# Sixteen-bit transposes moved from TensorE to transposing DMAs in a two-path attention kernel

## The chip, the cores and the metric

The kernel runs on one core of a Trainium2 chip. A core has TensorE (PE: matrix products and transposes through the array, with a separate row PEld for the loading of weights), VectorE (DVE), ScalarE (ACT), GpSimd (POOL) and SyncE (SP), which issues the DMAs here. Each engine runs its own instructions in order; semaphores tie the engines together. Products are written to PSUM, everything else lies in SBUF; the inputs, the output and scratch tensors lie in DRAM, and 16 DMA engines move data between DRAM and SBUF. The metric is the device time of one execution in microseconds.

## The reference

The input x has 2048 rows of 640. Two attention paths with 32 heads of 20 columns are computed from it and mixed by a gate per row.

```python
x = A_x
g = _sigmoid((x * gate_w).sum(-1, keepdims=True))
a = _A_ref(x, A_wqkv, A_w_phi, A_wo)
b = _B_ref(x, B_wq, B_wk, B_wv, B_wo, B_beta)
return g * a + (1 - g) * b
```

Path A is linear attention. Each head maps q and k by a 20x20 matrix and takes the softmax of the result and of its negative (40 features); kv and z are sums over all rows, and the output is num/den:

```python
phi_q = jnp.concatenate([_softmax(pq, axis=-1), _softmax(-pq, axis=-1)], axis=-1)
kv = jnp.einsum('bhsf,bhsd->bhfd', phi_k, v)
z = jnp.einsum('bhsf->bhf', phi_k)
o = num / den
```

Path B works in four segments of 512 rows. Inside a segment it is causal softmax attention; beside it stands a memory M, z that collects phi(k) v of the earlier segments, with phi(t) = t + 1 for t > 0 and exp(t) otherwise; both outputs are mixed by a gate per head:

```python
p = _softmax(logits, axis=-1)
a_dot = jnp.einsum('bhqk,bhkd->bhqd', p, vs)
o = g * a_mem + (1.0 - g) * a_dot
M = M + jnp.einsum('bhld,bhle->bhde', pk, vs)
```

Each path ends with a product by its own 640x640 output matrix.

## The kernel before

Rows are cut into 16 chunks of 128 (`sc`), four chunks to a segment (`s`); the 32 heads are handled in 8 groups of four (`g`), a head padded from 20 to 32 columns so that four heads fill 128 partitions. All matrix products with x need x transposed; `xT` holds it whole, 640 columns in five blocks of 128.

**Opening.** The DMAs are issued from SP in the order of the code: the first four chunks of x, the weights `WvA` and `wnat_k`, the rest of x, `wnat_q`, then the weights of path B. `x_transpose` (L207 to L214) turns one chunk: five PE transposes against an identity matrix into one PSUM tile, and one DVE copy into `xT`. `fold_tr` and `fold_mm` multiply the A weights of k, later of q, by `w_phi`.

**Chunk loop of path A (L325 to L336).** For each chunk: `a1_v(sc+2)` (values and the gate logit), `a1_k(sc)` (exponents of both signs on ACT, sums on DVE, the scaling into `EkN` on POOL), the transpose of chunk sc+4, a piece of the q fold from chunk 3 on, and `a1_kv(sc-2)`, which adds to kv and z.

**k and v of path B.** `b_k` (L361) makes one chunk of k: two products of 320 columns, each copied by DVE into the padded `kpad` tile (L369) and, for the first three segments, passed through exp by ACT (`ek`, L372); `phik` is then min(max(k, 0) + 1, exp(k)). `b_v` does the same for the values. Segment 0 is done ahead of the head loop.

**Head loop (L644).** One step k handles head group g of segment s; there are 32 steps, and work of the previous group is woven in. `b_q` makes the transposed q of the next group, with `eq` and `phiq` for the memory; `b_kT` (L409) transposes four 128x128 blocks of `kpad` on PE and copies them to `kT` on DVE (L415). `b_qk` (L420) computes scores in three parts, (chunk 0), (chunks 1 and 3), (chunk 2), into two PSUM tiles `st`; ACT takes the exponent into `PT` (L434) and POOL masks the diagonal blocks (L438). `b_pv` multiplies by the values (`nd`), `b_mem` reads and updates the memory (`am`, `mz`, L454), and `b_epi` writes the group's part of `oB`.

**Fill.** The other work goes between these: `b_k` and `b_v` of the next segment, path A's queries (`a3_pq`, `a3_num`, which ends in `oA`), and the output. `fin_tr` (L547) transposes a block of `oA` or `oB` on PE with a DVE copy into `oT` (L554); `fin_mm` (L557) multiplies ten such pieces by `WoA` and `WoB`, ACT copies the result to `osb`, and SP stores it. Every unit of fill has a position on the axis of steps, made by `place` from a list of knots; in step k, after each third of the scores, all units with a position below k plus 0.37, 0.74 or 1.0 are written out.

**What sets the order.** PE is scheduled by hand: its order is the order of the code. On the other engines and on SP a scheduler sets the order when the program is built, and each engine then keeps it. Four PSUM buffers (tag "w", pool `psw`) serve all products and transposes except the scores and the sums of path A; a product waits until an older user of its buffer has been read.

Of the kernel before, what the change touches and what calls it, by code (L numbers as in the profile page):

```python
# [15 lines left out]
def kernel(  # L16
# [15 lines left out]
    nc = tc.nc  # L32
# [26 lines left out]
    bkw = ctx.enter_context(tc.tile_pool(name="bkw", bufs=2))  # L59
    psw = ctx.enter_context(tc.tile_pool(name="psw", bufs=4, space=PSUM))  # L60
# [14 lines left out]
    x_nat = [apool.tile([P, 4, D], BF16, name=f"x_nat{i}") for i in range(4)]  # L75
# [17 lines left out]
    nc.sync.dma_start(out=x_nat[0][:, 0:2], in_=xv[:, 0:2, :])  # L93
# [4 lines left out]
    nc.sync.dma_start(out=x_nat[0][:, 2:4], in_=xv[:, 2:4, :])  # L98
    wload(WvA[:, :, 0:D], A_wqkv[:, 2 * D:3 * D])
    wload(wnat_k, A_wqkv[:, D:2 * D])  # L100
    for i in range(1, 4):
        nc.sync.dma_start(out=x_nat[i], in_=xv[:, 4 * i:4 * i + 4, :])
# [3 lines left out]
    wq_st = []  # L106
    for c in range(KC):
        w = a1w.tile([P, D], BF16, name="wq_st", bufs=2)
        nc.sync.dma_start(out=w, in_=B_wq[c * P:(c + 1) * P, :])
        wq_st.append(w)  # L110
    wload(WoA, A_wo)
    wload(WoB, B_wo)
    nc.sync.dma_start(out=beta_b, in_=B_beta.partition_broadcast(P))
# [33 lines left out]
    kpad2, phik2, vB2 = [], [], []  # L147
    for b in range(2):
        kp = bres.tile([P, 4, H, 32], BF16, name=f"kpad{b}")
        pk = bres.tile([P, 4, H, 32], BF16, name=f"phik{b}")  # L150
        vb = bres.tile([P, 4, H, V1], BF16, name=f"vB{b}")
        nc.gpsimd.memset(kp[:, :, :, DH:32], 0.0)
        nc.gpsimd.memset(pk[:, :, :, DH:32], 0.0)
        nc.gpsimd.memset(vb[:, :, :, DH:V1], 1.0)
        kpad2.append(kp)
        phik2.append(pk)
        vB2.append(vb)
# [49 lines left out]
    def x_transpose(sc):  # L207
        tp = wtile("xtp", BF16)
        for c in range(KC):
            nc.tensor.transpose(out=tp[:, c * P:(c + 1) * P],  # L210
                                in_=x_nat[sc // 4][:, sc % 4, c * P:(c + 1) * P],
                                identity=ident_b)
        nc.vector.tensor_copy(out=xT[:, :, sc * P:(sc + 1) * P],
                              in_=tp[:, 0:D].rearrange("p (c k) -> p c k", k=P))  # L214
# [110 lines left out]
    for sc in range(NCH):  # L325
        if sc + 2 < NCH:
            a1_v(sc + 2)
        a1_k(sc)
        if sc + 4 < NCH:
            x_transpose(sc + 4)  # L330
        if 3 <= sc < 3 + NG6:
            fold_tr(fq, sc - 3)
        if 9 <= sc < 9 + KC:
            fold_mm(fq, sc - 9)
        if sc >= 2:
            a1_kv(sc - 2)  # L336
# [24 lines left out]
    def b_k(s, c):  # L361
        kp, pk = kpad2[s % 2], phik2[s % 2]
        sc = 4 * s + c
        ek = bkw.tile([P, D], BF16, name="ek")
        rk = bkw.tile([P, D], BF16, name="rk", bufs=1)
        for hf in range(2):
            ps = wtile("kb_ps")
            mm_x(ps[:, 0:320], sc, WkB, 320 * hf, 320 * hf + 320)
            nc.vector.tensor_copy(out=kp[:, c, hf * 16:hf * 16 + 16, 0:DH],  # L369
                                  in_=ps[:, 0:320].rearrange("p (h d) -> p h d", d=DH))  # L370
            if s < NSEG - 1:
                nc.scalar.activation(out=ek[:, hf * 320:hf * 320 + 320], in_=ps[:, 0:320],  # L372
                                     func=ACT.Exp)
        if s < NSEG - 1:
            nc.vector.tensor_scalar(out=rk.rearrange("p (h d) -> p h d", d=DH),
                                    in0=kp[:, c, :, 0:DH], scalar1=0.0, scalar2=1.0,
                                    op0=ALU.max, op1=ALU.add)
            nc.vector.tensor_tensor(out=pk[:, c, :, 0:DH],
                                    in0=rk.rearrange("p (h d) -> p h d", d=DH),
                                    in1=ek.rearrange("p (h d) -> p h d", d=DH), op=ALU.min)  # L380
# [9 lines left out]
    def b_q(s, g):  # L390
        ps = wtile("qb_ps")
        for c in range(KC):
            nc.tensor.matmul(ps, lhsT=WqB[:, c, 4 * g:4 * g + 4, :],  # L393
                             rhs=xT[:, c, s * L:(s + 1) * L],
                             start=(c == 0), stop=(c == KC - 1))
        qT = bw.tile([P, L], BF16, name="qT", bufs=2)
        nc.vector.tensor_copy(out=qT, in_=ps)  # L397
        phiq = None
        if s > 0:
            eq = bw.tile([P, L], BF16, name="eq", bufs=1)  # L400
            nc.scalar.activation(out=eq, in_=ps, func=ACT.Exp)  # L401
            rq = bw.tile([P, L], BF16, name="rq")
            nc.vector.tensor_scalar(out=rq, in0=qT, scalar1=0.0, scalar2=1.0,
                                    op0=ALU.max, op1=ALU.add)
            phiq = bw.tile([P, L], BF16, name="phiq", bufs=3)
            nc.vector.tensor_tensor(out=phiq, in0=rq, in1=eq, op=ALU.min)
        return qT, phiq

    def b_kT(s, g):  # L409
        ps = wtile("kT_ps", BF16)  # L410
        for c in range(4):
            nc.tensor.transpose(out=ps[:, c * P:(c + 1) * P],
                                in_=kpad2[s % 2][:, c, 4 * g:4 * g + 4, :], identity=ident_b)
        kT = bw.tile([P, L], BF16, name="kT", bufs=2)
        nc.vector.tensor_copy(out=kT, in_=ps[:, 0:L])  # L415
        return kT
# [37 lines left out]
    def b_mem(s, g, phiq):  # L454
        tm = None
        if s > 0:
            am = wtile("am_ps")
            for j in range(4):
                nc.tensor.matmul(am[:, j * 84:(j + 1) * 84], lhsT=phiq[:, j * P:(j + 1) * P],
                                 rhs=Mbd[:, g].rearrange("p i e -> p (i e)"), start=True, stop=True)  # L460
            tm = b_norm(am, s, g, Cm, "m")
        if s < NSEG - 1:
            mz = wtile("mz_ps")
            for c in range(4):
                nc.tensor.matmul(mz[:, 0:84], lhsT=phik2[s % 2][:, c, 4 * g:4 * g + 4, :],
                                 rhs=vB2[s % 2][:, c, 4 * g:4 * g + 4, :],
                                 start=(c == 0), stop=(c == 3))
            nc.vector.tensor_tensor(out=Msb[:, g], in0=mz[:, 0:84].rearrange("p (i e) -> p i e", e=V1),
# [24 lines left out]
    segs = [Seg() for _ in range(NSEG)]  # L493

# [12 lines left out]
    def a3_num(s, qc, half):  # L507
# [33 lines left out]
        if qc == 0 and half == 0:  # L541
            segs[s].oA = boA.tile([P, 4, D], BF16, name="oA", bufs=3)
        nc.gpsimd.tensor_tensor(  # L543
            out=segs[s].oA[:, qc, h0 * DH:(h0 + nh) * DH].rearrange("p (h d) -> p h d", d=DH),
            in0=ts[:, 0, 0:nh, :], in1=ts[:, 1, 0:nh, :], op=ALU.add)

    def fin_tr(s, qc, X):  # L547
        o = segs[s].oA if X == 0 else segs[s].oB
        tp = wtile("otp", BF16)
        for k5 in range(KC):  # L550
            nc.tensor.transpose(out=tp[:, k5 * P:(k5 + 1) * P], in_=o[:, qc, k5 * P:(k5 + 1) * P],  # L551
                                identity=ident_b)
        oT = bw.tile([P, KC * P], BF16, name=f"oT{X}")
        nc.vector.tensor_copy(out=oT, in_=tp[:, 0:D])  # L554
        segs[s].oT[qc, X] = oT

    def fin_mm(s, qc, hf):  # L557
# [5 lines left out]
        for X, Wo in enumerate((WoA, WoB)):  # L563
            for k5 in range(KC):
                nc.tensor.matmul(ps[:, 0:320], lhsT=segs[s].oT[qc, X][:, k5 * P:(k5 + 1) * P],  # L565
# [27 lines left out]
    def fill_fin(s):  # L593
        tr = [[(0.3, lambda qc=qc, X=X: fin_tr(s, qc, X)) for X in range(2)] for qc in range(4)]
        mm = [[(0.68, lambda qc=qc, hf=hf: fin_mm(s, qc, hf)) for hf in range(2)]
              for qc in range(4)]
        u = tr[0] + []
        for qc in range(4):
            for hf in range(2):
                if qc < 3:  # L600
                    u.append(tr[qc + 1][hf])
                u.append(mm[qc][hf])
        return u
# [17 lines left out]
    for s, (p0, p1) in enumerate(((9.01, 17), (17.01, 25), (25.4, 32))):  # L621
        fill += place(fill_fin(s), ((0, p0), (1, p1)))
    fill.sort(key=lambda v: v[0])

    first = fill_bkv(0)
    for t, (_, u) in enumerate(first):
        u()
        if t == 1:
            a1_kv(NCH - 2)
        if t == 4:  # L630
            a1_kv(NCH - 1)
            a1_state()
# [8 lines left out]
    cur = (b_q(0, 0), b_kT(0, 0))  # L641
    prev = None
    SHARE = (0.37, 0.74, 1.0)
    for k in range(NG):  # L644
        s, g = divmod(k, G)
        if g == 0:
            segs[s].oB = boA.tile([P, 4, D], BF16, name="oB")
            segs[s].oT = {}
        (qT, phiq), kT = cur
        PT = bpt.tile([P, 4, 1280], BF16, name="PT")  # L650
        nd = None
        for t, cs in enumerate(((0,), (1, 3), (2,))):
            b_qk(qT, kT, PT, cs)
            if t == 0 and k + 1 < NG:
                nq = b_q(*divmod(k + 1, G))
            if t == 1 and k + 1 < NG:
                nxt = (nq, b_kT(*divmod(k + 1, G)))
            if prev is not None:
# [6 lines left out]
                else:  # L665
                    b_pv(ps_, pg_, pPT, [3], nd)
                    b_epi(ps_, pg_, nd, tm, segs[ps_].oB)
            while fill and fill[0][0] < k + SHARE[t]:
                fill.pop(0)[1]()
        prev = (s, g, PT, phiq)  # L670
        if k + 1 < NG:
            cur = nxt
    ps_, pg_, pPT, pphi = prev
# [4 lines left out]
    for _, u in fill_fin(NSEG - 1):  # L678
        u()
# [29 lines left out]
```

The softmax here doesn't subtract the row's maximum and nothing guards it: scores larger than these inputs give would overflow.

## Time and profile before

| | before |
|---|---|
| median time | 439.85 us (four runs, 438.72 to 439.86) |
| profiled span | 438.1 us |
| busy PE, ACT, DVE, POOL | 363.4, 274.7, 261.0, 210.4 us |
| mean granted TensorE clock | 0.941 |
| DRAM read and written | 9.21 and 2.62 MB |
| x_transpose, 16 chunks | 80 PE transposes, 16 DVE copies (median 492 ns) |
| kT, 32 groups | 128 PE transposes, 32 DVE copies (416 ns) |
| output blocks, 32 | 160 PE transposes, 32 DVE copies (483 ns) |

A page of the profile gives busy time per engine, the span in 40 equal slices (digits are tenths busy), the chain of work that ended last, followed back from the last instruction, and groups of instructions with their busy time, mean duration and the idle time of their engine before them. Matrix products overlap in the array, so the duration of one (219 ns for a transpose) is longer than the distance from one to the next. "A <- B" in the table of waits means that engine A stood idle until B was done. "issue" is idle time for which the profile shows no cause. A name such as `L551` is line 551 of the kernel before.

### The profile page before, as it was taken

What the parts mean: (1) busy time and instruction counts of PE and PEld (TensorE: products, weight loads), DVE (VectorE), ACT (ScalarE), POOL (GpSimd) and SP (SyncE); (2) the same over time, 40 slices, a digit from 0 to 9 for tenths busy, and PEclk for the clock granted to TensorE, in tenths of its full rate; (3) what the DMA queues carried; (4) which work ended last, traced back from release to release, by engine and by line L of the source; (5) the groups of instructions that cost most, each with busy time, mean ns of one, the idle gap of its engine ahead of it and who ended that gap; (6) DMA issues with size and microseconds to landing.
All of it is one profiled execution on the core that took longest, in us unless ns stands there. A gap on an engine that the chain in (4) does not pass through costs nothing.

```text
span 438.1 us, 10470 instructions
## 1 busy us (share of the span) xinstructions
PE 363.4 (83%) x4257; PEld 235.2 (54%) x4289; DVE 261.0 (60%) x680; ACT 274.7 (63%) x515; POOL 210.4 (48%) x365
## 2 busy tenths in 40 slices
PE   1899999797987687788988888898886788787686
PEld 1677877573454343455655455564554454445365
DVE  6477766896367453677665566665666456555431
ACT  1566666525687466777766677676676886765502
POOL 9047776950355444544463434554354545444510
PEclk9999999989899796899998999999999998988669
DMA  8960000000000000000000000000000000000001
GB/s 250 363 224 9 4 1 1 1 0 1 2 0 2 2 1 0 1 2 2 16 4 14 16 2 16 1 16 2 17 16 1 16 1 16 17 2 15 13 14 51
DMA packets 10610, 12.49 MB, mean 29 GB/s; under 512 B 1347, under 2 KB 10563, under 8 KB 10563
## 3 DMA queue, kind: packets, MB, share of 16 engines
q1 hardware_dynamic: 10563, 11.83, 8.2%
q8 instruction: 33, 0.54, 0.5%
q14 instruction: 14, 0.11, 0.1%
HBM read 9.21 MB, written 2.62 MB: 27 GB/s over the span
## 4 chain that ended last, share of the span: by engine, by line
PE 52%; ACT 19%; DVE 14%; POOL 9%; issue 4%; DMA 2%; SPq 0%; POOLq 0%; DVEq 0%; ACTq 0%
ACT PT L434 12%; PE o_ps L565 10%; PE pq_ps L500 6%; PE qb_ps L393 5%; PE vb_ps L231 4%; PE st L428 4%; PE va_ps L231 4%; PE kb_ps L231 4%; PE nd_ps L448 4%; POOL PT L438 3%; PE ka_ps L231 3%; DVE ts L538 2%; PE acc L271 2%; PE otp L551 2%; ACT eq L401 2%
## 5 line engine op out<-in xcount | busy, mean ns | idle before, releaser
L434 ACT ACTIVATE PT<-st 128x1024 bf16<-128x1024 f32 (+1 forms) x192 | 158.7, 885 | 21.7 <-PE st L428 19.6
L438 POOL TENSOR_SCALAR_AFFINE_SELECT PT<-PT 128x512 bf16<-128x512 bf16 x128 | 80.7, 642 | 114.6 <-ACT PT L434 98.8
L231 PEld LDWEIGHTS <-xT 128*128 128x128 bf16 x640 | 62.0, 100 | 32.3 <-issue 6.8
L428 PE MATMUL st<-qT,kT 32*128 32x128 bf16 (+3 forms) x512 | 44.5, 311 | 15.2 <-ACT PT L434 13.0
L397 DVE CAST qT<-qb_ps 128x512 bf16<-128x512 f32 x32 | 22.1, 691 | 46.0 <-PE qb_ps L393 45.9
L259 POOL TENSOR_TENSOR EkN<-Ek,krec 128x1280 bf16<-128x1280 bf16 x16 | 37.9, 2366 | 18.8 <-DVE krec L258 17.3
L448 PE MATMUL nd_ps<-vB,PT 128*128 128x21 bf16 x1280 | 42.4, 173 | 4.9 <-DVE ts L538 2.0
L448 PEld LDWEIGHTS <-PT 128*128 128x128 bf16 x1280 | 38.2, 97 | 10.8 <-POOL rr L529 3.8
L393 PE MATMUL qb_ps<-xT,WqB 128*128 128x512 bf16 x148 | 42.0, 404 | 1.8 <-DVE ts L538 0.8
L543 POOL TENSOR_TENSOR oA<-ts 128x360 bf16<-128x360 f32 (+1 forms) x32 | 27.6, 861 | 31.1 <-DVE ts L538 27.6
L565 PEld LDWEIGHTS <-oT 128*128 128x128 bf16 x320 | 31.5, 104 | 15.4 <-issue 1.7
L500 PE MATMUL pq_ps<-xT,WqA 128*128 128x512 bf16 x100 | 32.4, 420 | 8.6 <-DVE ts L538 3.1
L569 ACT CAST osb<-o_ps 128x320 bf16<-128x320 f32 x32 | 13.6, 426 | 39.5 <-PE o_ps L565 39.3
L428 PEld LDWEIGHTS <-kT 32*128 32x128 bf16 x512 | 14.0, 92 | 42.1 <-issue 37.1
L503 ACT ACTIVATE Eq<-pq_ps 128x512 bf16<-128x512 f32 x24 | 14.3, 597 | 28.6 <-PE pq_ps L500 28.4
L565 PE MATMUL o_ps<-WoA,oT 128*128 128x320 bf16 x160 | 29.9, 322 | 2.1 <-DVE ts L538 1.4
L518 PE MATMUL num_ps<-KVZ,Eq 128*128 128x132 bf16 (+1 forms) x192 | 18.5, 220 | 15.1 <-DVE ts L538 5.8
L231 PE MATMUL vb_ps<-WvB,xT 128*128 128x320 bf16 x160 | 27.2, 319 | 3.7 <-DVE ts L538 2.3
L538 DVE TENSOR_TENSOR ts<-num_ps,cs 128x360 f32<-128x360 f32 (+1 forms) x64 | 28.2, 483 | 1.9 <-DVE cs L533 0.2
L565 PE MATMUL o_ps<-WoB,oT 128*128 128x320 bf16 x160 | 28.9, 314 | 0.0
L241 ACT CAST vA<-va_ps 128x320 bf16<-128x320 f32 x32 | 13.7, 427 | 22.0 <-PE va_ps L231 22.0
L251 ACT ACTIVATE Ek<-ka_ps 128x320 bf16<-128x320 f32 x64 | 23.0, 439 | 5.5 <-PE ka_ps L231 4.9
(114 smaller groups left out, 669.0 us busy)
## 6 DMA issues: line engine op xcount, KB each, us to landing
out_dram<-osb SPq DMA_DIRECT2D x16, 160.0 KB, 1.8
x_nat<-in_A_x_dram SPq DMA_DIRECT2D x3, 640.0 KB, 9.1
WvA<-in_A_wqkv_dram SPq DMA_DIRECT2D x1, 800.0 KB, 5.5
wnat_k<-in_A_wqkv_dram SPq DMA_DIRECT2D x1, 800.0 KB, 7.3
wnat_q<-in_A_wqkv_dram SPq DMA_DIRECT2D x1, 800.0 KB, 11.3
WkB<-in_B_wk_dram SPq DMA_DIRECT2D x1, 800.0 KB
WvB<-in_B_wv_dram SPq DMA_DIRECT2D x1, 800.0 KB, 11.5
wq_st<-in_B_wq_dram SPq DMA_DIRECT2D x5, 160.0 KB, 7.6
```

The costliest lines, as they stand in the source:

```text
L231: nc.tensor.matmul(ps, lhsT=xT[:, c, sc * P:(sc + 1) * P], rhs=W[:, c, lo:hi], start=(c == 0), stop=(c == KC - 1))
L251: nc.scalar.activation(out=Ek[:, sgn, 320 * hf:320 * hf + 320], in_=ps[:, 0:320], func=ACT.Exp, scale=1.0 if sgn == 0 else -1.0)
L259: nc.gpsimd.tensor_tensor(out=EkNs[sc % 4][:, 0:1280].rearrange("p (h f) -> p h f", f=DH), in0=Ek.rearrange("p s (h f) -> p (s h) f", f=DH ...
L393: nc.tensor.matmul(ps, lhsT=WqB[:, c, 4 * g:4 * g + 4, :], rhs=xT[:, c, s * L:(s + 1) * L], start=(c == 0), stop=(c == KC - 1))
L428: nc.tensor.matmul(st2[i // 2][:, i % 2, o:o + n], lhsT=kT[r:r + 32, c * P:(c + 1) * P], rhs=qT[r:r + 32, c * P:L], start=True, stop=True, ...
L434: nc.scalar.activation(out=PT[:, 2 * pr:2 * pr + 2, base:base + w], in_=st2[pr][:, :, 0:w], func=ACT.Exp, scale=SCALE_B)
L438: nc.gpsimd.affine_select(out=view, in_=view, pattern=[[0, 4], [1, P]], compare_op=ALU.is_ge, fill=0.0, base=0, channel_multiplier=-1)
L448: nc.tensor.matmul(nd[:, j * 84 + i * V1:j * 84 + (i + 1) * V1], lhsT=PT[:, i, o:o + P], rhs=vb[:, c, 4 * g + i, :], start=(j == 0 and i = ...
L500: nc.tensor.matmul(ps, lhsT=WqA[:, c, g * 120:g * 120 + P], rhs=xT[:, c, s * L:(s + 1) * L], start=(c == 0), stop=(c == KC - 1))
L538: nc.vector.tensor_tensor(out=ts[:, sgn, 0:nh, :], in0=pss[sgn][:, :, 0:DH], in1=cs[:, sgn, 0:nh, None].to_broadcast([P, nh, DH]), op=ALU. ...
L543: nc.gpsimd.tensor_tensor(out=segs[s].oA[:, qc, h0 * DH:(h0 + nh) * DH].rearrange("p (h d) -> p h d", d=DH), in0=ts[:, 0, 0:nh, :], in1=ts ...
L565: nc.tensor.matmul(ps[:, 0:320], lhsT=segs[s].oT[qc, X][:, k5 * P:(k5 + 1) * P], rhs=Wo[:, k5, hf * 320:hf * 320 + 320], start=(n == 0), s ...
```

## The change

The purpose is to take transposes of 16-bit data off PE, with their PSUM buffers and DVE copies, and to have them made by the DMA engines, which can transpose a block on its way from DRAM to SBUF.

- **x.** Chunks 4 to 15 are read from DRAM by 12 transposing DMAs straight into `xT`. Chunks 0 to 3 stay on PE. The five `wq_st` loads and `beta_b` move up in the queue, ahead of these DMAs; `wnat_q` and the B weights follow them.
- **kT.** `b_k` writes its padded chunk (128x1024) to a DRAM scratch `kd` and reads it back transposed into `kT2`, which holds the 8 groups of one segment; there are two of them, and three rotating `kpad` chunks. `b_kT` is gone.
- **Output blocks.** `o_put` stores 128x640 blocks of `oA` and `oB` to the scratch `od`, `o_get` reads them back transposed into `oT`, 0.8 step ahead of the first product that uses them. For the last segment `oB` is still transposed on PE; its `oA` goes by DMA. The knots of the output work of the three segments in the loop begin 0.4 to 0.8 step later.
- **Exponents.** `ek` and `eq` read the 16-bit copies in SBUF instead of PSUM; `ek` is one instruction of 640 columns instead of two.
- **Memory.** `am` and `mz` share one PSUM bank; both products come before the normalisation.

```diff
-    for i in range(1, 4):
-        nc.sync.dma_start(out=x_nat[i], in_=xv[:, 4 * i:4 * i + 4, :])
+    for sc in range(4, NCH):
+        nc.sync.dma_start_transpose(out=xT[:, :, sc * P:(sc + 1) * P],
+                                    in_=x2[sc * P:(sc + 1) * P, :])
     wload(wnat_q, A_wqkv[:, 0:D])
...
-        if sc + 4 < NCH:
-            x_transpose(sc + 4)
...
-        kp, pk = kpad2[s % 2], phik2[s % 2]
+        kp, pk = kpads[(4 * s + c) % 3], phik2[s % 2]
...
-            if s < NSEG - 1:
-                nc.scalar.activation(out=ek[:, hf * 320:hf * 320 + 320], in_=ps[:, 0:320],
-                                     func=ACT.Exp)
+        rows = slice(c * P, (c + 1) * P)
+        nc.sync.dma_start(out=kd[s][rows, :], in_=kp.rearrange("p h d -> p (h d)"))
+        nc.sync.dma_start_transpose(out=kT2[s % 2][:, :, rows], in_=kd[s][rows, :])
         if s < NSEG - 1:
+            nc.scalar.activation(out=ek.rearrange("p (h d) -> p h d", d=DH), in_=kp[:, :, 0:DH],
+                                 func=ACT.Exp)
...
-            nc.scalar.activation(out=eq, in_=ps, func=ACT.Exp)
+            nc.scalar.activation(out=eq, in_=qT, func=ACT.Exp)
...
+        am = wtile("am_ps")
         if s > 0:
-            am = wtile("am_ps")
...
+        if s < NSEG - 1:
+            mz = am[:, 336:420]
...
+    def o_put(s, X, qc, src):
+        nc.sync.dma_start(out=od[s][X][qc * P:(qc + 1) * P, :], in_=src)
+
+    def o_get(s, X, qc):
+        rows = slice(qc * P, (qc + 1) * P)
+        oT = bw.tile([P, KC, P], BF16, name=f"oT{X}", bufs=4)
+        nc.sync.dma_start_transpose(out=oT, in_=od[s][X][rows, :])
+        segs[s].oT[qc, X] = oT
...
-    for s, (p0, p1) in enumerate(((9.01, 17), (17.01, 25), (25.4, 32))):
-        fill += place(fill_fin(s), ((0, p0), (1, p1)))
+    for s, (p0, p1) in enumerate(((9.8, 17.2), (17.8, 25.2), (25.8, 32))):
+        fin = place(fill_fin(s), ((0, p0), (1, p1)))
+        fill += fin
+        for X in range(2):
+            fill += [(max(fin[2 * qc][0] - 0.8, 8 * s + 8.7),
+                      lambda s=s, X=X, qc=qc: o_get(s, X, qc)) for qc in range(4)]
...
+    for qc in range(4):
+        o_get(NSEG - 1, 0, qc)
     ps_, pg_, pPT, pphi = prev
     tm = b_mem(ps_, pg_, pphi)
     nd = wtile("nd_ps")
     b_pv(ps_, pg_, pPT, [0, 1, 2, 3], nd)
     b_epi(ps_, pg_, nd, tm, segs[ps_].oB)
-    for _, u in fill_fin(NSEG - 1):
-        u()
+    fin_tr(NSEG - 1, 0)
+    for qc in range(4):
+        if qc < 3:
+            fin_tr(NSEG - 1, qc + 1)
+        for hf in range(2):
+            fin_mm(NSEG - 1, qc, hf)
```

## The prediction

> **What bounds the kernel now.** I read the busy shares and the chain of waits first, then the stretches by stage, then who waits for whom, then the timeline around the instructions that the change touches.
>
> ```profile
> PE 363.4 (83%) x4257; PEld 235.2 (54%) x4289; DVE 261.0 (60%) x680; ACT 274.7 (63%) x515; POOL 210.4 (48%) x365
> DMA  8960000000000000000000000000000000000001
> PE 52%; ACT 19%; DVE 14%; POOL 9%; issue 4%; DMA 2%; SPq 0%; POOLq 0%; DVEq 0%; ACTq 0%
> ```
>
> TensorE (PE) is the fullest engine and half of the chain that ends last. The DMA engines are idle after slice 3. By stage (columns: stretch and length, then busy us of PE, PEld, DVE, ACT, POOL, then granted clock, DMA share, GB/s):
>
> ```profile
> 24.00:84.00 60.00, 57.91 (x714) 45.49 (x711) 44.87 (x75) 40.32 (x112) 44.58 (x64) 1.00 0.10 30
> 84.00:103.00 19.00, 17.14 (x165) 12.02 (x167) 15.69 (x35) 3.93 (x11) 9.21 (x20) 0.91 0.01 2
> 103.00:417.00 314.00, 258.19 (x3130) 155.65 (x3158) 184.43 (x539) 218.43 (x368) 144.12 (x255) 0.93 0.02 8
> 417.00:438.00 21.00, 16.31 (x141) 11.80 (x137) 4.73 (x11) 3.41 (x8) 1.34 (x2) 0.84 0.09 32
> ```
>
> The chunk loop of path A (24 to 84) is filled by PE. The head loop (103 to 417, 32 steps of 314/32 = 9.8 us) has PE at 82% and ACT at 70%; its 56 us of PE idle time is the question. What PE waited for there:
>
> ```profile
> PE st L428 <- ACT PT L434: 13.0, 25, 1.4
> PE num_ps L518 <- DVE ts L538: 5.8, 3, 3.7
> PE num_ps L518 <- ACT eq L401: 5.1, 5, 1.0
> ```
>
> The other waits on `ACT eq` are 1.8, 1.0, 0.9 and 0.8 us, so 9.6 us in all; on the copies of kT and oT 0.9, 0.8, 0.3, 0.2 and 0.6, so 2.8 us; on `DVE ts` 16.9 us. These are PSUM buffers that come free late: the four "w" buffers are shared by every product and every transpose.
>
> **What the Trainium skill says.** "VectorE: DVE Perf Modes", section "The three transpose paths": a 128x128 bf16 transpose takes 390 ns on TensorE and 1309 ns by DMA. The TensorE figure is a latency: here five transposes in a row delay the next product by 0.28 us (timeline below), 56 ns each. "Advanced Engine Details and Errata", section "X-Bar Transpose (TRN2)": transposing DMAs are as fast as ordinary ones. "DMA: Bandwidth & Descriptors", section "Latency and other measured facts": 261 GB/s measured for a transposing DMA. The trace of before holds no transposing DMA, so nothing here confirms or denies the three. "SBUF — State Buffer", section "Who interferes with whom": a VectorE copy in a two-port mode and a GpSimd instruction exclude each other for the whole instruction. The trace agrees: a copy of 4 columns took 6.08 us while GpSimd ran its memsets.
>
> **Part 1: x transposed by DMA (chunks 4 to 15).** Removed: 12 groups of five transposes and 12 copies of 0.492 us on DVE.
>
> ```profile
> 428.65 0.44 PE L551 MATMUL otp<-ident_b,oA 128*128 128x128 bf16 x5
> 428.93 0.84 PE L565 MATMUL o_ps<-WoA,oT 128*128 128x320 bf16 x5
> ```
>
> From start to start the group costs PE 0.28 us. 12 x 0.28 = 3.4 us. A chunk lasted about 4.2 us, and GpSimd works 2.36 + 1.10 us of it with about 0.25 us between, so its floor is 3.7 us and it takes back a little: I take 3.0 us. Added: 12 transposing DMAs of 160 KB, then `wnat_q`, on one queue. The loads ahead of them are 3.0 MB, which at the 364 GB/s of 10 to 20 us and with the start end near 13 us. The next ones cost 160 KB / 261 GB/s = 0.63 us each at least (estimate from the DMA page) and 5 x 1.309 = 6.5 us at most (estimate from the VectorE page, blocks one after the other). Deadlines: chunk 4 is read after `a1_k(1)`, about 27 us; `wnat_q` is read by PE at 34.2 us in PE's own order, so a late one stops everything. With 2.5 us for its 800 KB, twelve transposes have (34.2 - 2.5 - 13)/12 = 1.55 us each before PE stands still. I take 0.63: two pages say it, and 1309 ns for 32 KB looks like a fixed latency, as 160 KB of output here takes 1.8 us to land. Then the last lands near 22 us and DMA costs nothing.
>
> The start: `beta_b` now comes early and in the built program DVE has `sig_b` ahead of `ident_b`, so the first four PE transposes wait for it. Before, DVE was held anyway:
>
> ```profile
> 5.47 6.08 DVE L135 CAST ind<-bd 128x4 bf16<-128x4 f32 x1
> 8.66 3.06 DVE L310 COPY WvA<-gtp 128x5 bf16<-128x5 bf16 x1
> ```
>
> They end when the memsets do (11.5 us). The kpad memsets shrink from two (1.37 + 1.69 us) to three of a quarter of the size, about 1.0 us together: 2 us less. DVE then starts near 9.5 us with 0.23 + 0.91 us more to do and five copies into WqB that wait for their loads (near 13 us). I take 0, within 2 us either way.
>
> **Part 2: kT by DMA.** Removed: 32 groups of four transposes, 0.24 us of PE each (253.63 to 253.87 us), and 32 DVE copies of 0.416 us. In the loop 31 x 0.24 = 7.4 us of PE and 12.9 us of DVE. Added: 16 writes of 256 KB to DRAM, each followed by a transposing DMA that waits for it on the in-order SP queue. The path is about 0.4 us issue, 1.8 us landing (as `out_dram<-osb`), 0.4 us issue, 1.8 + 1.0 us: 5.4 us. Segments 1 to 3 have their last k chunk about 2.9 steps (28 us) ahead. Segment 0 is the narrow one: its chunk 3 leaves DVE at 100.0 us and is needed by the second score group, 106.57 us before. It just fits; up to 3 us lost.
>
> **Part 3: output blocks by DMA.** Removed: seg 0 to 2, 24 groups x 0.28 = 6.7 us of PE and 24 copies x 0.485 = 11.6 us of DVE; in the tail four groups, 1.1 us. Added: put, wait, get on SP. The get of oB comes at step 8s+8.7, the first final product at 8s+9.8: about 10 us for a 5 us path. In the tail the four oA gets are queued before the last head's work and oB stays on PE, so no round trip stands at the end. SP is in order: a get that waits for its put holds the stores queued behind it, and ACT waits for a store only when both `osb` buffers are out, two blocks later (18 us). I cost these at 2 us.
>
> **Part 4: eq and ek read SBUF; am and mz share a bank.** `eq` no longer holds the PSUM buffer of q: the 9.6 us of PE waits on it are open to saving, I take half, since the next buffer may be late too: 4.8 us. `ek` becomes one instruction of 640 instead of two of 320: from 439 ns (320) and 597 (512) a slope of 0.82 ns, so 0.70 instead of 0.88 us, 12 times, 2 us of ACT beside other work. One bank fewer per head; b_norm of `am` now waits for four more products (0.15 us), nothing.
>
> **Sum.** Loop: PE loses (7.4 + 6.7)/0.93 clock = 15.2 us of work; as PE is busy 82% of the stage, that share counts: 12.5. Copies' waits 2.8; `ts` waits fall with DVE's load, 24.5 of 184 us: 13% of 16.9 = 2.2; eq 4.8. Less 2 + 3 for new waits: 17.3. With the opening 3.0 and the tail 1.1: 21.4, so 439.85 - 21.4 = 418.5 us.
>
> **The rivals.**
> - A, off the path: the loop is really set by the circle of scores, exponent (ACT, 70%), mask and value product. For: `ACT PT` is the largest wait of PE and the largest line of the chain, 12%. Against: only 13 of 56 us of idle time. Then a third of the loop's gain comes: 439.85 - 3 - 1.1 - 5.8 = 430.
> - B, the transposing DMA is slow (1.309 us a block): x takes 78 us, `wnat_q` lands near 94 instead of 33, so the opening is 57 us longer; segment 0's kT, 4 x 10.5 us, adds some 25; a segment needs 4 x 10.5 + 8 x 6.5 = 94 us of DMA against 78 of loop, 15 more. About 530 us. For: the one block price there is. Against: two pages' bandwidths.
> - C, new waits through the in-order queue: 12 output blocks each stop PE 2 us, four segment starts 1 us, and 0 at the start turns into 2: 418.5 + 30 = about 448, slower than before. For: every get stands behind a wait of 2 us, about 44 of them. Against: leads of one step and more.
>
> **How the numbers follow.** Forecast 0.56, A 0.20, B 0.11, C 0.12, and 0.01 for no change between them. Faster 0.76, same 0.02, slower 0.22. The range begins at 404 (all PE work and all waits on eq gained, no new wait: 15.2 + 2.8 + 9.6 + 2.2 in the loop and 4.5 elsewhere give 405.5) and ends at 446, below which lie A and the milder half of C; B and the rest are the 2 in 10 left out.
>
> **What would show it.** Right: no PE wait on a DMA over 2 us; the time between first chunks falls from 4.2 to near 3.9 us; the score loop's PE busy time falls by 14 to 17 us; waits on eq nearly gone; transposing DMAs under 1.5 us apart on SP. Wrong: PE idle at `wnat_q` near 34 us or at xT, long rows "PEld oT <- DMA" or "kT <- DMA", ACT waiting at `osb`, or a head loop as long as before with ACT fuller. A granted clock below 0.93 in the loop would eat the gain without any of these.

## The result and the profile after

| | before | after |
|---|---|---|
| median of all runs | 437.97 us (16 runs, 436.58 to 439.86) | 411.57 us (10 runs, 408.12 to 412.46) |
| ratio, 95% interval | | 0.9386 [0.9364, 0.9409] |
| profiled span, mean clock | 438.1 us, 0.941 | 409.8 us, 0.942 |

The change makes the kernel 6.1% faster, 26.4 us between the medians, 28.3 between the profiled spans. The forecast was 418.5 us; the range 404 to 446 holds the time. A ratio leaves out an execution that took over 1.5% more than the fastest one of its kernel, which here is one run, 435.11 us of e1. Line numbers in a profile are those of that run's own kernel. The busy shares, the slices of the DMA engines and the chain that ended last, of the page of after:

```profile
PE 341.1 (83%) x3930; PEld 216.0 (53%) x3961; DVE 231.2 (56%) x608; ACT 271.4 (66%) x503; POOL 209.3 (51%) x366
DMA  7989000035120122236112115621110152100411
PE 54%; ACT 20%; POOL 11%; DVE 9%; issue 4%; POOLq 0%; DVEq 0%; ACTq 0%
```

PE lost 22 us and DVE 30, but PE is still at 83%: the span shrank with it. The DMA engines, idle after slice 3 before, are now in use to the end, though far from full. PE has 31 records fewer than PEld (3930 against 3961; before 4257 against 4289). Each product loads its weights once (in the head loop of e7 below both counts are 2927), so these are missing records, in both traces about equally many, and the difference of the two PE times can be used.

To place the time I cut both executions at the same events: the first product `ka`, the first `kb`, the first score `st`, the first transpose `otp` of the tail. Stretches of before, then of after (stretch and length, busy us of PE, PEld, DVE, ACT, POOL, granted clock, DMA share, GB/s):

```profile
22.70:85.80 63.10, 60.25 (x749) 47.44 (x748) 45.98 (x76) 41.21 (x114) 46.14 (x69) 1.00 0.12 37
85.80:102.60 16.80, 15.72 (x136) 10.86 (x135) 14.74 (x34) 3.93 (x11) 7.64 (x15) 0.90 0.01 2
102.60:417.40 314.80, 258.96 (x3145) 156.20 (x3177) 184.43 (x539) 218.43 (x368) 144.51 (x255) 0.93 0.02 8
417.40:438.10 20.70, 15.91 (x125) 11.40 (x121) 4.73 (x11) 3.41 (x8) 0.94 (x2) 0.83 0.09 32
```

```profile
22.80:81.90 59.10, 56.71 (x689) 44.01 (x687) 39.04 (x56) 40.73 (x113) 45.73 (x68) 1.00 0.28 83
81.90:97.00 15.10, 13.90 (x136) 10.00 (x135) 13.10 (x33) 3.54 (x7) 8.08 (x16) 1.00 0.44 123
97.00:389.90 292.90, 243.20 (x2902) 142.57 (x2932) 164.98 (x484) 215.83 (x360) 145.00 (x255) 0.93 0.24 61
389.90:409.80 19.90, 15.12 (x106) 10.16 (x102) 2.89 (x7) 3.41 (x8) 0.90 (x2) 0.81 0.18 51
```

| stage | before | after | difference |
|---|---|---|---|
| start to first ka | 22.7 | 22.8 | +0.1 |
| chunk loop of path A (ka to kb) | 63.1 | 59.1 | -4.0 |
| k and v of segment 0 (kb to st) | 16.8 | 15.1 | -1.7 |
| head loop (st to tail's otp) | 314.8 | 292.9 | -21.9 |
| tail | 20.7 | 19.9 | -0.8 |

The k and v of segment 0 ran at a clock of 0.90 before and 1.00 after. Over all the runs this stretch follows the clock and not the place where kT is made: 15.1 to 15.6 us at 1.00 (15.3 in e1, which still has every transpose on PE), 16.2 at 0.94, 16.8 and 16.9 at 0.90. So most of its 1.7 us is no gain of the change. The head loop's PE busy time fell from 258.96 to 243.20 us (-15.8) and PE's idle time in it from 55.8 to 49.7 (-6.1); the granted clock is 0.93 in both. PE's largest waits in the head loop of after (waiting line, releaser: us in all, times, longest):

```profile
PE st L426 <- ACT PT L432: 18.7, 36, 1.9
PE num_ps L522 <- DVE ts L542: 5.1, 2, 4.0
PE qb_ps L400 <- DVE ts L542: 2.6, 3, 1.4
PE vb_ps L238 <- DVE Msb L470: 2.4, 3, 1.3
...
PE num_ps L522 <- DVE Msb L470: 1.3, 1, 1.3
```

The rows on `eq` and on the copies of kT and oT are gone. No row of PE names a DMA: every transpose by DMA was in time. Part of the gain was given back in two other rows: the exponent `PT` (13.0 before, 18.7 now) and `Msb`, which was 0.5 us and is 4.5 now, two rows of 0.4 that are not shown included. The memory's sum now lies in the bank of `am`, and that buffer stays taken until DVE has added it to `Msb`.

The queue itself, first its three transposing lines (ns min/median/max on SP, first and last start), then median us from issue to landing:

```profile
L111 SPq DMA_TRANSPOSE xT<-in_A_x_dram x12: 1276/1276/2657, 8.5 to 26.0; - x12
L378 SPq DMA_TRANSPOSE kT<-kd x16: 1232/1232/1677, 86.2 to 296.6; - x16
L559 SPq DMA_TRANSPOSE oT<-od x28: 1199/1202/1980, 149.2 to 390.2; - x28
```
```profile
kd<-kpad SPq DMA_DIRECT2D x16, 256.0 KB, 2.5
od<-oA SPq DMA_DIRECT2D x16, 160.0 KB, 1.8
oT<-od SPq DMA_TRANSPOSE x28, 2.8
kT<-kd SPq DMA_TRANSPOSE x16, 3.2
xT<-in_A_x_dram SPq DMA_TRANSPOSE x12, 3.9
```

A transposing DMA holds SP for 1.2 us or more, about the same for 160 and 256 KB, where an ordinary one mostly takes 0.3 to 0.6 us, and in the median lands 2.8 to 3.9 us after its issue.

### The profile page after: what moved, and what is told of

Same layout as the page of the kernel before. It is cut to its first block, busy times and chain, and to the rows that moved or that the text cites. A ratio compares the mean times of both kernels' runs of the same rounds, so it can differ in the third digit from the quotient of the medians.

```text
span 409.8 us, 9889 instructions
## 1 busy us (share of the span) xinstructions
PE 341.1 (83%) x3930; PEld 216.0 (53%) x3961; DVE 231.2 (56%) x608; ACT 271.4 (66%) x503; POOL 209.3 (51%) x366
## 3 DMA queue, kind: packets, MB, share of 16 engines
q1 hardware_dynamic: 59091, 29.41, 28.1%
## 4 chain that ended last, share of the span: by engine, by line
PE 54%; ACT 20%; POOL 11%; DVE 9%; issue 4%; POOLq 0%; DVEq 0%; ACTq 0%
ACT PT L432 15%; PE o_ps L579 11%; PE qb_ps L400 6%; PE va_ps L238 5%; PE st L426 5%; PE vb_ps L238 5%; PE pq_ps L504 5%; PE ka_ps L238 4%; PE kb_ps L238 4%; POOL PT L436 4%; PE nd_ps L446 3%; PE acc L278 3%; DVE ts L542 1%; DVE qT L404 1%; ACT osb L583 1%
## 5 line engine op out<-in xcount | busy, mean ns | idle before, releaser
L432 ACT ACTIVATE PT<-st 128x1024 bf16<-128x1024 f32 (+1 forms) x192 | 158.5, 884 | 18.9 <-PE st L426 17.5
L238 PEld LDWEIGHTS <-xT 128*128 128x128 bf16 x640 | 60.8, 99 | 30.4 <-DVE Msb L470 2.9
L426 PE MATMUL st<-qT,kT 32*128 32x128 bf16 (+3 forms) x512 | 48.5, 311 | 21.3 <-ACT PT L432 18.7
L446 PEld LDWEIGHTS <-PT 128*128 128x128 bf16 x1280 | 36.7, 96 | 14.1 <-issue 6.4
L579 PEld LDWEIGHTS <-oT 128*128 128x128 bf16 x320 | 32.4, 105 | 19.9 <-issue 4.1
L426 PEld LDWEIGHTS <-kT 32*128 32x128 bf16 x512 | 15.7, 92 | 50.9 <-issue 47.9
L479 DVE RECIPROCAL rd<-nd_ps 128x16 f32<-128x16 f32 x32 | 8.0, 249 | 36.9 <-PE nd_ps L446 36.9
L263 DVE TENSOR_REDUCE ksum<-Ek 128x64 f32<-128x1280 bf16 x16 | 23.7, 1482 | 8.2 <-ACT Ek L258 7.6
L400 PEld LDWEIGHTS <-WqB 128*128 128x128 bf16 x160 | 13.9, 101 | 23.3 <-issue 12.9
```

The source lines that it names most:

```text
L238: nc.tensor.matmul(ps, lhsT=xT[:, c, sc * P:(sc + 1) * P], rhs=W[:, c, lo:hi], start=(c == 0), stop=(c == KC - 1))
L400: nc.tensor.matmul(ps, lhsT=WqB[:, c, 4 * g:4 * g + 4, :], rhs=xT[:, c, s * L:(s + 1) * L], start=(c == 0), stop=(c == KC - 1))
L426: nc.tensor.matmul(st2[i // 2][:, i % 2, o:o + n], lhsT=kT[r:r + 32, c * P:(c + 1) * P], rhs=qT[r:r + 32, c * P:L], start=True, stop=True, ...
L432: nc.scalar.activation(out=PT[:, 2 * pr:2 * pr + 2, base:base + w], in_=st2[pr][:, :, 0:w], func=ACT.Exp, scale=SCALE_B)
L446: nc.tensor.matmul(nd[:, j * 84 + i * V1:j * 84 + (i + 1) * V1], lhsT=PT[:, i, o:o + P], rhs=vb[:, c, 4 * g + i, :], start=(j == 0 and i = ...
L579: nc.tensor.matmul(ps[:, 0:320], lhsT=segs[s].oT[qc, X][:, k5, :], rhs=Wo[:, k5, hf * 320:hf * 320 + 320], start=(n == 0), stop=(n == 2 * ...
```

## The experiments

The theory: PE's transposes and the PSUM buffers and copies that they held were on the path of the head loop, and the DMAs hide. The rivals: the gain came from one small part (the x opening, or `eq`); only one of the three freed resources counts; the queue is near the path. Unless said otherwise, a difference is the difference of two ratios (0.9386 for the changed kernel) times the time of before in the same call (438.35 to 439.22 us). Nothing of the computation is left out in any of these kernels.

### Parts alone, on the kernel before

`eq` alone (e1), which reads the copy instead of PSUM:

```diff
-            nc.scalar.activation(out=eq, in_=ps, func=ACT.Exp)
+            nc.scalar.activation(out=eq, in_=qT, func=ACT.Exp)
```

> The kernel before with one line changed: eq reads qT in SBUF instead of the PSUM buffer of q. Theory of the prediction: half of the 9.6 us that PE waited on eq comes back, 4.8 us faster than before. Rival: the next buffer is late as well and the wait only moves, less than 1 us.

Measured: 0.9812 [0.9749, 0.9875], 8.2 us faster than before. This rests on three runs (427.22 to 431.85 us) that had clocks of 0.948 to 0.951, where before had 0.937 to 0.949. At like clocks the gain is 5 to 6 us: 430.56 and 431.85 at 0.948 against 436.73 at 0.949, and 435.11 against 440.09, both at 0.937. All of part 4 (e2): beside `eq`, one `ek` from SBUF and `mz = am[:, 336:420]`.

> The kernel before with the whole of part 4 (eq and ek read SBUF, am and mz share a bank), every transpose still on PE. Theory: about 5 us faster, nearly all from eq. Rival: sharing the bank frees a PSUM buffer per head as well, 8 us or more.

Measured: 435.55 us, 0.9936 [0.9915, 0.9957], 2.8 us faster, where 5 was expected. So `ek` with the shared bank gives back part of what `eq` alone brings: 5.4 us by the ratios (the two intervals leave 2.5 to 8.3), about 3 at like clocks. The profiles agree: PE is idle for 46.3 us of the head loop in e1 and for 50.1 in e2. Which of the two does it wasn't separated; PE's waits on `Msb`, 1.1 us in e1 and 3.7 in e2, speak for the bank. Part 1 alone (e3), x by DMA, with its order of loads:

```diff
-        if sc + 4 < NCH:
-            x_transpose(sc + 4)
+    for sc in range(4, NCH):
+        nc.sync.dma_start_transpose(out=xT[:, :, sc * P:(sc + 1) * P],
+                                    in_=x2[sc * P:(sc + 1) * P, :])
```

> The kernel before with part 1 alone (x chunks 4 to 15 by transposing DMAs, loads reordered). Theory: 12 groups of transposes on PE, 3.4 us, and nothing lost to the queue: 3 to 4 us faster than before. Rival: the later start of the first transposes and the loads behind the DMAs take it back, under 1.5 us.

Measured: 436.52 us, 0.9932 [0.9904, 0.9959], 3.0 us faster, as expected. Its chunk loop is 4.0 us shorter, as in the changed kernel, but its first `ka` comes 1.8 us later than before (24.5). The two parts make 5.8 of about 27 us, which leaves some 21 for kT and the output blocks.

### Parts undone, on the changed kernel

kT back on PE (e4), with `b_kT` and its DVE copy in place of `kd`; the output blocks back on PE (e5), with `fin_tr` for both paths and the old knots:

```diff
-        nc.sync.dma_start(out=kd[s][rows, :], in_=kp.rearrange("p h d -> p (h d)"))
-        nc.sync.dma_start_transpose(out=kT2[s % 2][:, :, rows], in_=kd[s][rows, :])
...
+                nxt = (nq, b_kT(*divmod(k + 1, G)))
```

> The changed kernel with kT made on PE and copied by DVE again, no scratch for k. Theory: 7.4 us of PE at clock 0.93 in the head loop, all of it counting now that the stage lost 15.8 us of PE work and 21.9 us of time, with some waits on buffers, and 1.3 us ahead of the loop: 9 to 11 us slower than the changed kernel. Rival: the narrow deadline of segment 0 and the trips through the queue ate part of the gain: under 6 us slower.

> The changed kernel with all output blocks transposed on PE and copied by DVE again, with the old positions of this work. Theory: 6.7 us of PE at clock 0.93 in the loop, some waits on buffers and 1.1 us in the tail: 8 to 10 us slower than the changed kernel. Rival: the put and get in one queue cost as much as they save: under 4 us slower.

Measured: e4 424.88 us, 0.9711 [0.9657, 0.9764], 14 us slower than the changed kernel; e5 423.12 us, 0.9652 [0.9603, 0.9702], 12 us slower. Both lie above what was expected. In the head loop of e4 PE is busy for 7.2 us more than in e7, the same loop without products added and with every PE record there (see below), and the loop is 12.0 us longer; in e5 it is 6.4 and 7.9. So beside the PE work waits came back, more of them with kT. The two make 26 us together against 21 left after parts 1 and 4; with some 3 us of uncertainty on each, this doesn't show that the parts help each other.

### Which freed resource counts

Each transposed block freed three things: PE time, DVE time, one turn of a "w" buffer. Three kernels put one of them back into the changed kernel, at the same 56 places, beside the q and the output products and not where the old transposes stood, with results that nothing uses: PE time (e6: four idle products of 128 columns for each q, five for each of 24 output products, in tiles that are there anyway), DVE time (e7: 56 reductions) and buffers (e11: a product of 4 columns into a tile of its own, and a copy of 4 columns).

```diff
+            nc.tensor.matmul(ps[:, c * P:(c + 1) * P], lhsT=ident_b, rhs=ident_b,
+                             start=True, stop=True)
```
```diff
+            nc.vector.tensor_reduce(out=dd, in_=qT[:, 0:352], axis=AX.X, op=ALU.max)
```
```diff
+        sl = wtile("sl")
+        nc.tensor.matmul(sl[:, 0:4], lhsT=ident_b, rhs=ind, start=True, stop=True)
+        sd = bw.tile([P, 4], F32, name="sd", bufs=4)
+        nc.vector.tensor_copy(out=sd, in_=sl[:, 0:4])
```

> The changed kernel with only the PE time of the removed transposes put back: four idle 128x128 products ahead of each q product and five ahead of each output product of the first three segments, into buffers that are overwritten at once; no further PSUM buffer, no DVE copy. Theory that PE work itself counts: 14.1 us at clock 0.93, 12 to 15 us slower than the changed kernel. Rival, that the buffers and copies counted: under 6 us slower.

> The changed kernel with only the DVE time of the removed copies put back: a reduction of 352 elements after each q copy and one of 320 at each output product of the first three segments, about 0.42 us each, 56 in all, read by nobody. Theory: DVE at 56% of the loop has room, 2 to 4 us slower than the changed kernel. Rival, that DVE's queue delayed PE's buffers: 8 us slower or more.

> The changed kernel with only the PSUM buffers of the removed transposes put back: at each of the 56 places one product of 4 columns into a buffer of its own and a DVE copy of 4 columns that frees it. Theory: 2 to 5 us slower than the changed kernel. Rival, that the four shared buffers were the real bound: 8 us slower or more.

| put back | median us | ratio [95%] | slower than the changed kernel by |
|---|---|---|---|
| PE time | 424.93 | 0.9633 [0.9574, 0.9692] | 10.8 us |
| DVE time | 419.16 | 0.9541 [0.9482, 0.96] | 6.8 us |
| buffer turns | 426.5 | 0.9684 [0.9629, 0.974] | 13.1 us |

Each difference is uncertain by some 3 us, so that the first and the last aren't told apart. PE time came out just below what was expected, DVE time above it.

The head loop of the three (columns as above), in this order:

```profile
96.40:400.00 303.60, 257.89 (x3173) 156.53 (x3173) 164.76 (x484) 216.23 (x360) 145.24 (x255) 0.94 0.24 59
```
```profile
99.10:395.60 296.50, 246.90 (x2927) 142.96 (x2927) 182.01 (x540) 215.83 (x360) 144.29 (x255) 0.94 0.24 60
```
```profile
96.70:403.00 306.30, 251.88 (x2983) 145.02 (x2983) 172.07 (x539) 215.98 (x360) 145.91 (x255) 0.93 0.24 59
```

In these traces no PE record is missing (3173 and 3173, and so on), so the DVE kernel, which adds no product, shows the complete PE time of the loop: 246.9 us, and so 46.0 us of idle time in the 292.9 of the changed kernel. In e6 PE time was raised by 11.0 us, the loop by 10.7, and 45.7 us are idle: in this profile the idle time takes up nothing of the added work. The clock of that run was higher (0.951 against 0.942 over the whole span), so 11.0 understates the work: four idle products in a row hold PE for 0.23 us (257.15 to 257.38 us), 58 ns each, which is some 14 us for all 248. Against 14 the run times, 10.8 us and 3 either way, leave 0.6 to 1.0 as the share that counts. DVE time adds no PE time and 3.6 us to this loop; the rest of its 6.8 lies ahead of the loop, or in the lower clocks of the other three runs (0.923 to 0.935). The buffers add 5.0 us of PE time but 13.4 to the loop: about 8 us of it is waiting. PE's rows of that kernel show where:

```profile
PE num_ps L526 <- DVE qT L408: 4.7, 12, 0.5
PE o_ps L588 <- DVE sd L583: 3.9, 8, 0.9
```

In the second row a product waits for the copy of 4 columns, in the first for the copy of q, whose buffer comes round sooner with one more user. But the small copy also stands ahead of the copy of q on DVE, and the copies add 7 us of DVE time, so 13 us is more than buffers alone. The theory had them at 2 to 5 us and was too low; the rival (8 or more) fits better. All three count, and they do not add up: 31 us against 22 of loop, so they overlap.

### How near the queue is

Each of the 12 x transposes issued twice (e8); each of the 44 read-backs of kT and oT issued twice (e9).

```diff
-    for sc in range(4, NCH):
+    for sc in list(range(4, NCH)) * 2:
```
```diff
+        for _ in range(2):
+            nc.sync.dma_start_transpose(out=oT, in_=od[s][X][rows, :])
```

> The changed kernel with every transposing DMA of x issued twice, the second time over the first, so that readers wait for the second. One takes 1.57 us of the queue here. Theory of the deadline: twelve more put wnat_q about 19 us later, near 50 us, where PE asks for it at 33 us: 14 to 18 us slower than the changed kernel, with PE idle at xT and wnat_q. Rival: there is slack, under 3 us.

> The changed kernel with every transposing read of kT and of the output blocks issued twice, 44 more DMAs. Theory: these lie off the path, with leads of 5 us and more: within 2 us of the changed kernel. Rival, that the in-order queue is close to the path: 8 us slower or more, with PE waiting on oT or kT and ACT at osb.

Measured: e8 428.53 us, 0.978 [0.9736, 0.9825], 17 us slower, as expected. Its first row below is the wait that the prediction's rival B feared: PE at the late `wnat_q`.

```profile
PE wtp L191 <- DMA wnat_q<-in_A_wqkv_dram: 9.9, 1, 9.9
...
PE va_ps L238 <- DMA xT<-in_A_x_dram: 2.8, 1, 2.8
```

The two waits make 12.7 us, but from the first `ka` to the first `kb` it is 76.6 us instead of 59.1, 17.5 more. The other 4.8 us are PE's own work (61.6 us busy instead of 56.7) at a mean clock of 0.88 instead of 1.00. From 48 to 54 us, after the long wait, the clock was 0.50, and ten products of a chunk took nearly twice as long as those of the next chunk:

```profile
50.42 2.84 PE L238 MATMUL va_ps<-WvA,xT 128*128 128x320 bf16 x10
56.13 1.53 PE L238 MATMUL va_ps<-WvA,xT 128*128 128x320 bf16 x10
```

So here a wait of PE cost more than its own length.

e9: 443.98 us, 1.0121 [1.0081, 1.0161], 32 us slower than the changed kernel and 1.2% slower than before; I had expected no more than 2 us. First PE's waits, then SP's timeline around one step (start, us, instruction):

```profile
PE o_ps L581 <- DMA oT<-od: 22.5, 3, 10.2
...
PE st L427 <- DMA kT<-kd: 5.6, 1, 5.6
```
```profile
161.00 1.21 SPq L561 DMA_TRANSPOSE oT<-od  x1
162.30 4.54 SPq L379 DMA_TRANSPOSE kT<-kd  x2
```

A pair into the same tile takes 4.5 us of SP, not 2.5, since the second waits for the first to land. So the load is larger than doubled, and the test is rougher than meant. The four waits on DMAs make 28.1 us of the 31.2 by which the head loop is longer; PE also works at a clock of 0.89 there and is busy for 5.9 us more. Still it shows the limit: the queue of the changed kernel is no free resource. The first to be late is kT of segment 0 (the 5.6 us end at 108.85 us), the outputs lose the most.

### A faster version

The start still waits 10.5 us for `ident_b`, as predicted: on DVE it stands behind `sig_b`, which ends with GpSimd's memsets (here at 10.0 us). Timeline of DVE, changed kernel:

```profile
7.02 2.97 DVE L356 TENSOR_SCALAR sig_b<-sig_b 128x32 f32<-128x32 f32 x1 [6.08 <-ACT sig_b L355]
```

e10 moves `beta_b` to the end of the loads, the first four copies of `xT` and the gate column to ACT, and in the tail the `WoA` halves of the first chunk's two products ahead of the transposes of `oB`. e12 is the same with `beta_b` after the `wq_st` loads.

```diff
-    nc.sync.dma_start(out=beta_b, in_=B_beta.partition_broadcast(P))
...
+    nc.sync.dma_start(out=beta_b, in_=B_beta.partition_broadcast(P))
...
-        nc.vector.tensor_copy(out=xT[:, :, sc * P:(sc + 1) * P],
+        nc.scalar.copy(out=xT[:, :, sc * P:(sc + 1) * P],
...
+    for hf in range(2):
+        fin_mm(NSEG - 1, 0, hf, 0)
```

> The changed kernel with a better start and end: beta_b loaded last again, the copies of the first four x chunks and of the gate column on ACT, which does not wait for GpSimd's memsets; and in the tail the first two half products with WoA put ahead of the last transposes of oB. Theory: 1.7 us at the start (the first value product limited by the landing of WvA near 11 us instead of 12.8) and 1.6 us at the end, 3 us faster than the changed kernel. Rival: the fold of the k weights waits for wnat_k at 13.3 us and for DVE as before, under 1 us at the start.

> The kernel of the best-version run, with beta_b issued after the wq loads and ahead of the transposing DMAs, instead of last. Theory: the lost time of the best version was the in-order ACT standing 8.3 us at sig_b for the late beta; with beta early, the start gain (first four copies of xT on ACT instead of DVE behind the GpSimd memsets, 3 us) and the shorter end (WoA halves first, 2 us) are both kept: about 5 us faster than the changed kernel, 406 to 408 us, ratio near 0.927. Rival: the earlier start only moves PE's arrival at wnat_q, which lands where it did, so that the 3 us are lost in a wait there: within 2 us of the changed kernel.

Measured: e10 416.09 us, 0.9483 [0.9453, 0.9513], 4 us slower than the changed kernel although its first `ka` comes 3.1 us earlier. The wait had moved to ACT:

```profile
ACT sig_b L355 <- DMA beta_b<-in_B_beta_dram: 8.3, 1, 8.3
```

ACT's `sig_b` stood for the late `beta_b` ahead of the copies that PE needs, and PE waited 6.5 us for ACT (`wtp` for `vA`). From the first `ka` to the first `kb` it took 68.3 us instead of 59.1. The other 2.7 us are again PE's own work (59.4 us busy instead of 56.7) at a mean clock of 0.94 instead of 1.00. e12: 407.29 us, 0.9273 [0.9236, 0.9311], 5.0 us faster than the changed kernel (3 to 7 by both intervals). Its stretches, cut at the same events:

```profile
20.10:79.70 59.60, 56.85 (x688) 43.86 (x686) 39.04 (x56) 40.89 (x113) 45.68 (x68) 1.00 0.29 85
...
391.90:407.10 15.20, 11.88 (x91) 8.46 (x89) 1.97 (x4) 3.40 (x8) 0.00 (x0) 0.93 0.13 45
```

The first `ka` comes at 20.1 instead of 22.8, and `wnat_q` is then late by 0.4 us only. But the first score comes at 96.58, no more than 0.4 us earlier: k and v of segment 0 took 16.9 us at a clock of 0.90, where the changed kernel had 15.1 at 1.00. From there to the end are 310.5 us instead of 312.8; part of the tail's work now lies ahead of its first transpose, so the tail's own 15.2 us are not to be set against 19.9. The profiled execution was the slowest of six (408.82 us), so the trace doesn't show how the 5.0 us of the runs divide between start and end.

## Why the prediction was right, point by point

- **Direction and mechanism: right.** PE's work and the waits on its buffers bound the head loop; 21.9 of 28.3 us came from there (17.3 predicted). Rival A (the circle of scores and exponents, one third of the gain) falls by the time itself, 411.57 and not 430 us, and by e4 to e6: work put back on PE made the loop longer by about as much or more. Something of it is seen, though: the waits on `PT` grew by 5.7 us.
- **"as PE is busy 82% of the stage, that share counts: 12.5": the term that was most off.** Removed were 15.8 us (15.2 predicted, so the count and the price of 0.24 and 0.28 us a group were right), and PE's idle time in the loop didn't grow by any of it: it fell. This is 3.3 of the 7 us by which the sum of 21.4 fell short of 28.3. The profile of e6 says the same of work that is added, while its run times alone would also allow the 82%. A share of busy time is no probability that work is on the path: here the idle time was waits between products in a fixed order, and removed work moved what stood behind it.
- **Copies 2.8, `ts` 2.2, `eq` 4.8, less 5 for new waits: net 4.8, measured 6.1.** That the sum came near was luck, the single terms were not right. The rows on `ts` fell by 5.3 us (16.9 to 11.6). `eq` alone is worth 5 to 8, and `ek` with the shared bank gives 3 to 5 back, which I had costed at nothing ("b_norm of `am` now waits for four more products"): I looked at who waits for the four products, and not at how long the buffer stays taken. The new waits on DMAs were none, but those on `PT` and `Msb` grew by 9.7. The buffer turns, which the sum knew only as waits on named copies, seem to be worth more than their rows (e11).
- **Opening 3.0: 3.0 alone (e3), 4.0 in the chunk loop of after.** The price of the DMA was wrong, 1.57 us from start to start (12 in 18.82 us) and not 0.63. That is just above the 1.55 us that I gave as the limit before PE stands still, and above the 1.5 that I named as a sign of being right. What saved it is another wrong number, and that was luck: the transposes start at 8.45 us and not at 13, since SP only issues the loads and does not wait for them to land. SP's timeline of after:

```profile
8.45 18.82 SPq L111 DMA_TRANSPOSE xT<-in_A_x_dram  x12
27.31 0.58 SPq L94 DMA_DIRECT2D wnat_q<-in_A_wqkv_dram  x1
```

Of the Trainium skill, the claims "as fast as ordinary ones" and 261 GB/s (pages "Advanced Engine Details and Errata", section "X-Bar Transpose (TRN2)", and "DMA: Bandwidth & Descriptors", section "Latency and other measured facts") do not hold for one queue here: 160 KB in 1.57 us are 104 GB/s. Whether SP or the DMA engines set this wasn't separated: at least half of the 12 held SP for the shortest time of the row, 1.28 us, but from 20 to 26 us the engines were also 73% or more busy, at 93 to 143 GB/s. Rival B, blocks of 1.309 us one after the other (6.5 us for 160 KB), is farther off on the other side. The margin is thin: in e8 PE goes on 5.1 us after `wnat_q` is issued (43.28 to 48.41), which in after would be 32.4 us (an estimate), and PE reads it at 33.4.
- **Start, 0 within 2: right (+0.1), and for the reason given.** DVE was free at 10.0 us instead of 11.5 and had more to do first. In e3 and e4, which have the two large `kpad` memsets of before, the first `ka` comes at 24.5 and 24.7 us.
- **Path of kT, 5.4 us: right.** The write lands 2.5 us after the start of its issue and the transpose 3.2 after its own, 5.7 in the medians. For chunk 3 of segment 0 the write was issued at 94.98 us and the transpose at 97.03, landing near 100.2 (5.3 us); its scores start at 100.99 with no wait recorded. It "just fits", by less than a microsecond, and it is the first to be late in e9.
- **Rival C, the in-order queue: no such wait in the changed kernel.** But e9 makes it real with one more transfer for each. How much of the leads of 0.8 step is needed wasn't tried.
- **k and v of segment 0, -1.7 us, was not in the sum,** and rightly: at a clock of 1.00 the stretch takes 15.3 us in e1 and 15.1 in after. So at one clock the change is worth some 0.2 us there, and the rest of the 1.7 is the clock.
- **Tail 1.1: 0.8.**

## What to carry to other kernels

Price work on a hand-ordered engine that is 80% busy at its full time, and then count separately the PSUM buffer turns that go with it: 56 turns with little work in them (5 us of PE, 7 of DVE) cost 13 us here. When two uses are put into one buffer, ask how long it stays taken, not only who waits for the second. A transposing DMA cost its queue over a microsecond here, so count queue time up to the next load that the main engine needs, and start the transfers early rather than hope for bandwidth. Before a difference of a few microseconds is explained, set the granted clocks of the two stretches side by side.

## What the runs showed of the hardware

- Five transposes on PE cost 56 ns each in a row; four idle products of 128 columns in e6 58 ns each (0.23 us).
- After PE had waited 9.9 us (e8) and 6.5 us (e10), ten products of 320 columns took 2.84 us instead of 1.53.
- A transposing DMA of 128x640 held SP for 1.20 to 1.28 us in the median and one of 128x1024 for 1.23 us (16 bits each); 12 in a row started 1.57 us apart. A second one into the same tile waited for the first to land.
- `eq` from a 16-bit tile in SBUF takes 630 ns, from 32-bit PSUM it took 597: the gain of that edit is the buffer, not the exponent. `ek` of 640 columns takes 737 ns, against 2 x 437.
- The 32-column `sig_b` took 2.97 us on DVE, to 9.99 us, while GpSimd's memsets ended at 9.95. This agrees with the Trainium skill ("SBUF — State Buffer", section "Who interferes with whom"), which says that a DVE instruction in a two-port mode and one of GpSimd block each other; that this one is in such a mode no run shows.
